# Casting and turning the inputs block by block, with a rearranged opening, in a gated recurrence followed by a maxout layer

## The chip, the cores and the metric

The kernel runs on one core of one Trainium2 chip. The core has five engines, each with its own queue of instructions in program order: TensorE (PE, matrix multiplies), VectorE (DVE), ScalarE (ACT), GpSimd (POOL) and SyncE (SP, which here only issues transfers), and 16 DMA engines that they share. The metric is the time of one execution on the device, in microseconds (us).

## What is computed

`x` and `f_logit` are [4, 6144, 256] in float32, `w1` and `w2` are [256, 1024], `w_out` is [1024, 256].

```python
sig = 1 / (1 + exp(-f_logit))
f = lower_bound + (1 - lower_bound) * sig
i = 1 - f
h = 0
for t in range(6144):                 # for each of 4 sequences, 256 channels
    h = f[:, t] * h + i[:, t] * x[:, t]
    y[:, t] = h
g = maximum(y @ w1, y @ w2)           # y as 24576 tokens of 256
out = g @ w_out
```

The kernel rewrites this. With u = sigmoid(-f_logit), i is (1 - lower_bound) u and f is 1 - (1 - lower_bound) u. The factor (1 - lower_bound), `om` in the code, leaves the recurrence and is multiplied into the weights. The maximum is taken as h1 + relu(h2 - h1): one matmul with `wd` = om (w2 - w1) and a relu, and the linear part y (om w1 w_out) with a 256x256 matrix `w13` that is made once.

## The kernel before

The 24576 tokens are cut into 48 blocks of 512 tokens (`TB`), 12 to a sequence. For the scan and the matmuls a block must lie with its channels on the partitions, so it has to be turned. This is done in two ways.

Blocks 0 to 2 are loaded in float32 with tokens on the partitions (`load`, tiles `fn`, `xn`), gated there (`gate_nat` on ACT makes `un`, `drive_nat` on DVE makes `vn` = un xn) and turned on PE (`turn_pe`). Blocks 3 to 47 go through DRAM. `cast` has POOL issue two DMAs that write bfloat16 copies of the rows, `fs` and `xs`, to a scratch tile in DRAM; `turn_dma` has SP issue two transposing DMAs that bring them back as `fT` and `xT`. Block 3 is a chunk of its own, and then two blocks make a chunk (`CB = 2`). `cast_after_turn` keeps the two apart: POOL first copies one element of the `fT` just being turned into `held`, and so waits until it has landed, before it issues the next cast. The next turn waits for that cast. There are two pairs of scratch tiles (`NS`) and three buffers each for `fT` and `xT` (pool `turned`).

`gate` (ACT) makes `u` from `fT`, `drive` (DVE) makes `v` = u xT, `forget` makes `ff` = 1 - om u, and `scan` (DVE) runs the recurrence over a block, once for each half of the channels, from the last column of the block before.

The main loop runs over blocks j and eight slots `fc`. In a slot PE does `hidden(j, fc)`, two matmuls of 512 columns into a `dT` tile (pool `ps_d`, five banks), and half a token group of `project(j-1, .)`, five matmuls of 256 columns into a `psO` tile (`ps_o`, three banks). ACT turns `dT` into `rt` with the relu. `store` copies a `psO` tile to `osb` on DVE and has SP write it out, twice a block, at `fc` 0 and 4. All orders are written out by hand: `gate_of` says in which slot a block is gated, `turn_of` in which slot a chunk is turned. A gate that waits holds up what is behind it on ACT and DVE, relus among it; a turn that waits holds up the stores behind it on SP.

In the opening the weights come in quarters of their columns. For each quarter `diff` makes w2 - w1, `scale` multiplies by `om` into `wd`, and `turn_w1` turns w1 on PE for the linear matrix (`keep_w1` copies it out, `linear_weights` multiplies, `keep_linear` scales). `keep_warm` issues matmuls without use while data is awaited. At the end the last tokens are stored by `store_row`, one copy half on DVE and half on ACT.

Of the kernel before, what the change touches and what calls it, by code (L numbers as in the profile page):

```python
# [8 lines left out]
FP32 = mybir.dt.float32  # L9
BF16 = mybir.dt.bfloat16  # L10
ALU = mybir.AluOpType
AF = mybir.ActivationFunctionType
# [4 lines left out]
def kernel(  # L17
# [26 lines left out]
    CB = 2  # L44
    assert NBB % CB == 0
    chunks = [(NP, 1)] + [(j, CB) for j in range(NP + 1, NBLK, CB)]
    NCH = len(chunks)
    home = {j + o: (c, o) for c, (j, n) in enumerate(chunks) for o in range(n)}
    NS = 2
# [8 lines left out]
    ttpool = ctx.enter_context(tc.tile_pool(name="turned", bufs=3))  # L58
# [3 lines left out]
    opool = ctx.enter_context(tc.tile_pool(name="opool", bufs=4))  # L62
    PS = bass.MemoryType.PSUM
# [10 lines left out]
    w1n = wpool.tile([P, KC, DFF], FP32)  # L74
    w2n = wpool.tile([P, KC, DFF], FP32)
# [63 lines left out]
    def scan(j, h, t0=0, t1=TB):  # L139
# [18 lines left out]
    rows, chunk = {}, {}  # L158

    spare = {  # L160
        (k, name): scratch.tile([CB * TB, D], BF16, name=f"{name}{k}")
# [4 lines left out]
    def cast(c):  # L166
        j, n = chunks[c]
        b, k = divmod(j, NBB)
        rows[c] = []
        for name, src in (("fs", f_logit), ("xs", x)):  # L170
            t = spare[c % NS, name]
            nc.gpsimd.dma_start(  # L172
                out=t[0 : n * TB, :],
                in_=src[b, k * TB : (k + n) * TB, :],
                max_dma_last_dim=4096,
            )
            rows[c].append(t)

    def turn_dma(c):
        n = chunks[c][1] * TB  # L180
        for s in range(2):
            t = ttpool.tile([P, KC, CB * TB], BF16, name=("fT", "xT")[s])
            chunk[c, s] = t
            nc.sync.dma_start_transpose(out=t[:, :, 0:n], in_=rows[c][s][0:n, :])

    def gate(j):
        c, o = home[j]
        us[j] = midpool.tile([P, KC, TB], BF16, name="u")
        nc.scalar.activation(  # L189
            out=us[j][:],  # L190
            in_=chunk[c, 0][:, :, o * TB : (o + 1) * TB],
            func=AF.Sigmoid,
            scale=-1.0,
        )
        uT[j] = us[j]

    def drive(j):
        c, o = home[j]
        vT[j] = midpool.tile([P, KC, TB], BF16, name="v")
        nc.vector.tensor_tensor(  # L200
            out=vT[j][:],
            in0=us[j][:],
            in1=chunk[c, 1][:, :, o * TB : (o + 1) * TB],
            op=ALU.mult,
        )
# [4 lines left out]
    def unit(fc):  # L210
        return slice(fc * P, (fc + 1) * P)
# [61 lines left out]
    def store(j, g):  # L273
        osb = opool.tile([P, 2, D], FP32, name="osb")
        nc.vector.tensor_copy(out=osb[:], in_=pos[j, g, 0][:])  # L275
        r0 = j * TB + 2 * g * P
        nc.sync.dma_start(
            out=out[r0 : r0 + 2 * P, :].rearrange("(p r) d -> p r d", r=2), in_=osb[:]
        )

    def store_row(j, g, r):
        osb = opool.tile([P, 2, D], FP32, name="osb")
        ps = pos[j, g, r]
        nc.vector.tensor_copy(out=osb[:, 0, 0:P], in_=ps[:, 0, 0:P])
        nc.scalar.copy(out=osb[:, 0, P:D], in_=ps[:, 0, P:D])
        r0 = j * TB + 2 * g * P
        nc.sync.dma_start(
            out=out[r0 : r0 + 2 * P, :].rearrange("(p r) d -> p r d", r=2)[:, r, :],
            in_=osb[:, 0, :],
        )  # L290
# [4 lines left out]
    def weight_load(k, w, src):  # L295
        cols = slice(k * QF, (k + 1) * QF)
        nc.sync.dma_start(  # L297
            out=w[:, :, cols], in_=src[:, cols].rearrange("(h p) f -> p h f", p=P)
        )
# [25 lines left out]
    def scale(k, h):  # L325
        cols = slice(k * QF, (k + 1) * QF)
        nc.scalar.activation(
            out=wd[:, h, cols], in_=wdf[:, h, cols], func=AF.Copy, scale=om[:, h : h + 1]
        )

    pts = {}

    def turn_w1(k):
        pts[k] = ps_d.tile([P, 2, D], FP32, name="dT")
        for q in range(2):
            for h in range(KC):
                nc.tensor.transpose(
                    pts[k][:, q, h * P : (h + 1) * P],
                    w1n[:, h, unit(2 * k + q)],
                    ident[:],  # L340
                )

    def keep_w1(k):
        nc.scalar.copy(out=w1T[:, 2 * k : 2 * k + 2, :], in_=pts[k][:])
# [33 lines left out]
    gate_at = {NP: (1, 7), NP + 1: (3, 2), NP + 2: (3, 6), NP + 3: (5, 0), NP + 4: (5, 5)}  # L378
    gate_at |= {b: (b - 2, 5) for b in range(NP + 5, NBLK)}
    gate_of = {}  # L380
    for b, at in gate_at.items():
        gate_of.setdefault(at, []).append(b)
    turn_of = {(1, 3): 1}
    turn_of |= {(chunks[c][0] - 3, 5): c for c in range(2, NCH)}

    def cast_after_turn(c):

        last = chunks[c - 1][1] * TB - 1
        nc.gpsimd.tensor_copy(out=held[:], in_=chunk[c - 1, 0][:, KC - 1, last : last + 1])  # L389
        cast(c)  # L390

    with tc.manual_schedule():
# [4 lines left out]
        nc.scalar.dma_start(out=lbr[:], in_=lower_bound.rearrange("(h p) -> h p", p=P))  # L397
        load(0, 0, 0, 2)
        load(0, 1, 0, 2, nc.scalar)
        for k in range(2):  # L400
            weight_load(k, w1n, moe_w1)
            weight_load(k, w2n, moe_w2)
            if k == 0:
                load(0, 0, 2, 4)
                load(0, 1, 2, 4)
# [15 lines left out]
        keep_warm(6)  # L421
        keeps()
        keep_warm(2)


        gate_nat(0, 0, 2)
        drive_nat(0, 0, 2)
        for s in range(2):
            for q in range(2):
                turn_pe(0, s, q)  # L430
        forget(0, 0, 0, HB, on_act=True)
        forget(0, 1, 0, HB)
        for h in range(KC):
            scan(0, h, 0, HB)
        diff(0, 0, KC, nc.gpsimd)
        turn_w1(0)
        keep_warm(3)
        gate_nat(0, 2, 4)
        drive_nat(0, 2, 4)
        for s in range(2):  # L440
            for q in range(2, 4):
                turn_pe(0, s, q)
        scale(0, 0)
        forget(0, 0, HB, TB, on_act=True)
        forget(0, 1, HB, TB)
        scale(0, 1)
        keep_w1(0)
        for fc in range(2):
            hidden_cols(0, fc, 0, HB)
        for h in range(KC):  # L450
            diff(1, h, h + 1, nc.gpsimd)
# [3 lines left out]
        for h in range(KC):  # L455
            scale(1, h)
# [6 lines left out]
        keep_w1(1)  # L463
        for h in range(KC):
            diff(2, h, h + 1, nc.gpsimd)
        for h in range(KC):
            scale(2, h)
# [3 lines left out]
        turn_w1(2)  # L471
        for s in range(2, 4):
            for i in range(4):
                project_steps(0, i, s, s + 1)
        keep_w1(2)
        diff(3, 0, KC, nc.vector)
        for h in range(KC):
            scale(3, h)
        for fc in range(4, 6):
            hidden(0, fc, on_dve=(fc == 5))  # L480
        linear_weights(0, 4)
        turn_w1(3)
        gate_nat(1, 0, 2)
        drive_nat(1, 0, 2)
        keep_w1(3)


        for q in range(2):
            turn_pe(1, 0, q)
        for h in range(KC):  # L490
            forget(1, h, 0, HB, on_act=True)
        for fc in range(6, 8):
            hidden(0, fc, on_dve=(fc == 7))
# [14 lines left out]
        forget(1, 0, HB, TB, on_act=True)  # L508
        forget(1, 1, HB, TB)
# [6 lines left out]
        for i in range(4):  # L516
            project_steps(0, i, 8, 10)


        nc.gpsimd.tensor_copy(out=held[:], in_=ins[2][0][:, NQ - 1, D - 1 : D])  # L520
        cast(0)
        turn_dma(0)
        cast_after_turn(1)

        for j in range(1, NBLK + 1):
# [3 lines left out]
            for fc in range(FC):  # L529
                if j < NBLK:  # L530
                    hidden(j, fc, on_dve=(j == 1 and fc % 2 == 1))
# [5 lines left out]
                if j == 1:  # L537
                    if fc == 0:
                        gate_nat(2, 0, NQ)
                        drive_nat(2, 0, NQ)  # L540
                        store(0, 0)
                    if fc == 3:
                        store(0, 1)
                    if fc in (5, 6):
                        for q in range(NQ):
                            turn_pe(2, fc - 5, q)
                    if fc == 7:
                        for h in range(KC):
                            forget(2, h, on_act=True)
                        for h in range(KC):  # L550
                            scan(2, h)
# [15 lines left out]
                c = turn_of.get((j, fc))  # L567
                if c is not None:
                    turn_dma(c)
                    if c + 1 < NCH:  # L570
                        cast_after_turn(c + 1)
# [30 lines left out]
```

## Time and profile before

| | us |
|---|---|
| timed runs, median (lowest to highest of 3) | 402.17 (401.64 to 513.32) |
| the profiled execution | 400.45 |
| its span, first to last instruction | 398.7 |
| PE busy | 389.7 |
| ACT busy | 271.2 |
| DVE busy | 248.7 |
| POOL busy | 46.5 |

The profiled execution is one execution of its own. Its own time is 1.75 us more than its span. A row of a group or of the timeline gives the line of the code, the engine, the operation and what it writes from what. `PEld` is the loading of a stationary operand, `SPq` or `POOLq` an entry of a queue, such as the issue of a DMA. The row marked PE in the slices counts the tenths in which it was busy. A wait names the waiting engine and line, then what it waited for, the total, how many times, and the longest. The granted clock of TensorE was 1.0 throughout.

### The profile page before, as it was taken

To read this page: it belongs to the slowest core of one execution; us is meant where nothing else is said; L and a number is where in the kernel's file an instruction comes from. 1 tells how busy PE (TensorE), PEld (TensorE's weight loads), DVE (VectorE), ACT (ScalarE), POOL (GpSimd) and SP (SyncE) were. 2 spreads that over 40 slices of the span, in tenths; PEclk is the share of its full clock that TensorE was granted. 3 is DMA by queue.
4 is the path that set the end of the run, shared out by engine and by line. 5 is a ranking of instruction groups with operands and counts; after the bars stand their busy time and mean duration, and the time that the engine had idled before them with its cause. 6 is when DMAs were issued, how large, how long until landed. Compare 5 with 4: busy or idle time off the path is not lost.

```text
span 398.7 us, 7240 instructions
## 1 busy us (share of the span) xinstructions
PE 389.7 (98%) x2784; PEld 271.9 (68%) x2784; DVE 248.7 (62%) x353; ACT 271.2 (68%) x450; POOL 46.5 (12%) x82
## 2 busy tenths in 40 slices
PE   7989999999999999999999999999999999999996
PEld 4756676667776677766777667776677766777664
DVE  3677757765676577567656765765676567657621
ACT  3856767667766766676677667666766776676661
POOL 2420111011012020020110110110201101100000
PEclk9999999999999999999999999999999999999999
DMA  8979999999998999999999999999999999895122
GB/s 261 348 162 188 231 221 248 200 220 194 201 223 193 214 191 219 200 177 234 190 186 220 202 187 216 198 217 203 173 238 183 190 218 206 188 213 145 54 103 83
DMA packets 126359, 79.13 MB, mean 198 GB/s; under 512 B 96242, under 2 KB 102644, under 8 KB 126324
## 3 DMA queue, kind: packets, MB, share of 16 engines
q1 hardware_dynamic: 113792, 54.80, 54.2%
q0 software_dynamic: 12256, 23.60, 36.8%
q8 instruction: 22, 0.36, 0.4%
q10 hardware_dynamic: 276, 0.26, 0.2%
q14 instruction: 13, 0.11, 0.1%
HBM read 53.48 MB, written 48.76 MB: 256 GB/s over the span
## 4 chain that ended last, share of the span: by engine, by line
PE 87%; DMA 10%; DVE 1%; POOL 0%; issue 0%; ACTq 0%; SPq 0%; ACT 0%; DVEq 0%; POOLq 0%
PE psO L259 49%; PE dT L221 38%; DMA xs<-in_x_dram 2%; DMA fn<-in_f_logit_dram 2%; DMA w2n<-in_moe_w_dram 2%; DMA xT<-xs 1%; DMA xn<-in_x_dram 1%; DMA fs<-in_f_logit_dram 1%; DMA fT<-fs 1%; DVE y L148 1%; DVE v L200 0%; POOL fs L172 0%; ACTq L397 0%; DVE ff L135 0%; SPq L297 0%
## 5 line engine op out<-in xcount | busy, mean ns | idle before, releaser
L236 ACT ACTIVATE rt<-dT 128x512 bf16<-128x512 f32 x376 | 219.1, 596 | 112.5 <-PE dT L221 111.8
L221 PE MATMUL dT<-y,wd 128*128 128x512 bf16 (+1 forms) x772 | 227.3, 378 | 2.9 <-DVE rt L234 1.4
L259 PE MATMUL psO<-wob,rt 128*128 128x256 bf16 x1536 | 229.0, 273 | 0.2 <-DVE rt L234 0.2
L259 PEld LDWEIGHTS <-rt 128*128 128x128 bf16 x1536 | 150.2, 98 | 96.1 <-DVE rt L234 0.4
L148 DVE TENSOR_TENSOR_SCAN y<-ff,y,v 128x512 bf16<-128x512 bf16 x84 | 107.8, 1283 | 3.0
L200 DVE TENSOR_TENSOR v<-u,xT 128x1024 bf16<-128x1024 bf16 x45 | 31.1, 691 | 100.2 <-ACT u L189 91.7
L221 PEld LDWEIGHTS <-wd 128*128 128x128 bf16 x772 | 75.4, 98 | 15.1 <-issue 3.5
L275 DVE COPY osb<-psO 128x512 f32<-128x512 f32 x95 | 64.3, 678 | 29.2 <-PE psO L259 29.1
L259 PE MATMUL psO<-w,y 128*128 128x256 bf16 x384 | 72.8, 273 | 0.0
L389 POOL CAST held<-fT 128x1 f32<-128x1 bf16 x22 | 14.6, 663 | 286.5 <-DMA fT<-fs 286.5
L189 ACT ACTIVATE u<-fT 128x1024 bf16<-128x1024 bf16 x45 | 47.1, 1047 | 0.0
L259 PEld LDWEIGHTS <-y 128*128 128x128 bf16 x384 | 37.5, 98 | 4.4
L135 DVE TENSOR_SCALAR ff<-u,nom 128x512 bf16<-128x512 bf16 x90 | 30.3, 337 | 0.0
L172 POOL DMA_DIRECT2D fs<-in_f_logit_dram x23 | 12.8, 558 | 1.7 <-issue 1.5
L172 POOL DMA_DIRECT2D xs<-in_x_dram x23 | 12.7, 550 | 0.0
L148 DVE TENSOR_TENSOR_SCAN y<-ff,v 128x512 bf16<-128x512 bf16 x6 | 7.3, 1225 | 0.2
L234 DVE TENSOR_SCALAR rt<-dT 128x512 bf16<-128x512 f32 x8 | 5.3, 686 | 3.2 <-PE dT L221 3.2
L148 DVE TENSOR_TENSOR_SCAN y<-ff,y,dT 128x256 bf16<-128x256 bf16 (+1 forms) x8 | 6.6, 861 | 0.0
L370 PE MATMUL psO<-warm 128*128 128x512 bf16 x11 | 5.3, 629 | 1.2 <-DVE warm L418 1.2
L110 DVE TENSOR_TENSOR vn<-un,xn 128x512 bf16<-128x512 bf16 (+1 forms) x5 | 3.9, 788 | 3.3 <-ACT un L103 2.0
L131 ACT ACTIVATE ff<-dT,nom 128x256 bf16<-128x256 bf16 (+1 forms) x7 | 3.5, 536 | 3.1 <-PE dT L122 3.1
L318 POOL TENSOR_TENSOR wdf<-w2n,w1n 128x256 f32<-128x256 f32 (+1 forms) x5 | 4.1, 837 | 7.5 <-DMA w2n<-in_moe_w_dram 7.5
(34 smaller groups left out, 40.1 us busy)
## 6 DMA issues: line engine op xcount, KB each, us to landing
out_dram<-osb SPq DMA_DIRECT2D x95, 256.0 KB, 3.0
fs<-in_f_logit_dram POOLq DMA_DIRECT2D x22, 512.0 KB, 5.8
xs<-in_x_dram POOLq DMA_DIRECT2D x22, 512.0 KB, 9.2
fn<-in_f_logit_dram SPq DMA_DIRECT2D x4, 256.0 KB, 5.9
w1n<-in_moe_w_dram SPq DMA_DIRECT2D x4, 256.0 KB, 5.8
w2n<-in_moe_w_dram SPq DMA_DIRECT2D x4, 256.0 KB, 6.5
won<-in_moe_w_out_dram SPq DMA_DIRECT2D x2, 512.0 KB, 6.7
xn<-in_x_dram SPq DMA_DIRECT2D x3, 256.0 KB, 6.8
```

Of the source, the lines that this page charges most:

```text
L135: nc.vector.tensor_scalar(out=o, in0=i, scalar1=nom[:, h : h + 1], scalar2=1.0, op0=ALU.mult, op1=ALU.add)
L148: nc.vector.tensor_tensor_scan(out=ys[j][:, h, t0:t1], data0=ffs[j][:, h, t0:t1], data1=vT[j][:, h, t0:t1], initial=initial, op0=ALU.mult, ...
L172: nc.gpsimd.dma_start(out=t[0 : n * TB, :], in_=src[b, k * TB : (k + n) * TB, :], max_dma_last_dim=4096,)
L189: nc.scalar.activation(out=us[j][:], in_=chunk[c, 0][:, :, o * TB : (o + 1) * TB], func=AF.Sigmoid, scale=-1.0,)
L200: nc.vector.tensor_tensor(out=vT[j][:], in0=us[j][:], in1=chunk[c, 1][:, :, o * TB : (o + 1) * TB], op=ALU.mult,)
L221: nc.tensor.matmul(dts[j, fc][:, t0:t1], lhsT=wd[:, kc, unit(fc)], rhs=ys[j][:, kc, t0:t1], start=(t0 == 0 and kc == 0), stop=(t1 == TB an ...
L234: nc.vector.tensor_relu(out=rt[:], in_=dts[j, fc][:])
L236: nc.scalar.activation(out=rt[:], in_=dts[j, fc][:], func=AF.Relu)
L259: nc.tensor.matmul(ps, lhsT=lhsT, rhs=rhs, start=(s == 0 and (r == 0 or alone)), stop=(s == FC + KC - 1 and (r == 1 or alone)), skip_group ...
L275: nc.vector.tensor_copy(out=osb[:], in_=pos[j, g, 0][:])
L370: nc.tensor.matmul(idle[:].rearrange("p r d -> p (r d)"), lhsT=warm[:, 0:P], rhs=warm[:], start=True, stop=True,)
L389: nc.gpsimd.tensor_copy(out=held[:], in_=chunk[c - 1, 0][:, KC - 1, last : last + 1])
```

## The change

Casts and turns go block by block from block 3 on. There are three pairs of scratch tiles and five buffers each for `fT` and `xT`. A turn still waits for its cast, and the next cast for that turn, through `held`. Slots for turns and gates come from a formula: the turn of block b stands 13 slots ahead of its `hidden` at block 6, and the lead grows to 21 slots at block 18 and stays there; the gate stands five slots after the turn. Block 3's cast waits for the second half of block 1's `xn` rather than for block 2's `fn`.

In the opening `lbr` (the lower bound) moves from ACT's queue to SP's, behind the first load. `w1` is rounded to bfloat16 by `round_w1` before it is turned, on POOL for quarters 0, 2 and 3 and on ACT for quarter 1. `scale` runs partly on DVE, `diff` of quarter 2 moves from POOL to DVE and that of quarter 3 from DVE to POOL, some `forget` calls move to ACT, one `keep_w1` to DVE. Block 2 is gated and driven ahead of the main loop, its turning and its two scans are spread over block 1's slots, and block 0's outputs are copied on ACT. At the end, each of the two last rows is copied whole on DVE to a tile of its own.

```diff
-    CB = 2
-    chunks = [(NP, 1)] + [(j, CB) for j in range(NP + 1, NBLK, CB)]
-    NS = 2
+    NS = 3
...
-    ttpool = ctx.enter_context(tc.tile_pool(name="turned", bufs=3))
+    ttpool = ctx.enter_context(tc.tile_pool(name="turned", bufs=5))
...
+    def turn_dma(j):
+        for s, name in enumerate(("fs", "xs")):
+            t = ttpool.tile([P, KC, TB], BF16, name=("fT", "xT")[s])
+            turned[j, s] = t
+            nc.sync.dma_start_transpose(out=t[:], in_=spare[j % NS, name][:])
+
+    def cast_after_turn(j):
+        nc.gpsimd.tensor_copy(out=held[:], in_=turned[j - 1, 0][:, KC - 1, TB - 1 : TB])
+        cast(j)
...
     def store_row(j, g, r):
-        osb = opool.tile([P, 2, D], FP32, name="osb")
-        ps = pos[j, g, r]
-        nc.vector.tensor_copy(out=osb[:, 0, 0:P], in_=ps[:, 0, 0:P])
-        nc.scalar.copy(out=osb[:, 0, P:D], in_=ps[:, 0, P:D])
+        osb = lastpool.tile([P, D], FP32, name="row")
+        nc.vector.tensor_copy(out=osb[:], in_=pos[j, g, r][:, 0, :])
...
+    def round_w1(k, on_act=False):
+        cols = slice(k * QF, (k + 1) * QF)
+        o, i = w1b[:, :, cols], w1n[:, :, cols]
+        if on_act:
+            nc.scalar.copy(out=o, in_=i)
+        else:
+            nc.gpsimd.tensor_copy(out=o, in_=i)
...
-    gate_at = {NP: (1, 7), NP + 1: (3, 2), NP + 2: (3, 6), NP + 3: (5, 0), NP + 4: (5, 5)}
-    gate_at |= {b: (b - 2, 5) for b in range(NP + 5, NBLK)}
...
-    turn_of = {(1, 3): 1}
-    turn_of |= {(chunks[c][0] - 3, 5): c for c in range(2, NCH)}
+    turn_of, gate_of = {(1, 7): [NP + 1], (3, 2): [NP + 2]}, {(1, 7): [NP]}
+    for b in range(NP + 1, NBLK):
+        at = max(FC * (b - 2) + 3 - (2 * (b - 2 * NP)) // 3, FC * (b - 3) + 3)
+        if b > NP + 2:
+            turn_of.setdefault(divmod(at, FC), []).append(b)
+        if b == NP + 1:
+            at -= 3
+        gate_of.setdefault(divmod(at + 5, FC), []).append(b)
...
-        nc.scalar.dma_start(out=lbr[:], in_=lower_bound.rearrange("(h p) -> h p", p=P))
         load(0, 0, 0, 2)
         load(0, 1, 0, 2, nc.scalar)
+        nc.sync.dma_start(out=lbr[:], in_=lower_bound.rearrange("(h p) -> h p", p=P))
...
+        gate_nat(2, 0, NQ)
+        drive_nat(2, 0, NQ)
-        nc.gpsimd.tensor_copy(out=held[:], in_=ins[2][0][:, NQ - 1, D - 1 : D])
-        cast(0)
-        turn_dma(0)
-        cast_after_turn(1)
+        nc.gpsimd.tensor_copy(out=held[:], in_=ins[1][1][:, NQ - 1, D - 1 : D])
+        cast(NP)
+        turn_dma(NP)
+        cast_after_turn(NP + 1)
...
-                    hidden(j, fc, on_dve=(j == 1 and fc % 2 == 1))
+                    hidden(j, fc, on_dve=(j == 1 and fc in (1, 3, 6)))
...
                 if j == 1:
-                    if fc == 0:
-                        gate_nat(2, 0, NQ)
-                        drive_nat(2, 0, NQ)
-                        store(0, 0)
-                    if fc == 3:
-                        store(0, 1)
-                    if fc in (5, 6):
+                    if fc in (0, 2):
                         for q in range(NQ):
-                            turn_pe(2, fc - 5, q)
-                    if fc == 7:
+                            turn_pe(2, fc // 2, q)
+                    if fc == 2:
                         for h in range(KC):
                             forget(2, h, on_act=True)
-                        for h in range(KC):
-                            scan(2, h)
+                    if fc == 3:
+                        scan(2, 0)
+                    if fc == 6:
+                        scan(2, 1)
+                    if fc == 5:
+                        store(0, 0, on_act=True)
+                    if fc == 7:
+                        store(0, 1, on_act=True)
```

## The prediction, made before the changed kernel had run

> **What bounds the kernel now.** I began with busy time and the slices, to see which engine is full, and where.
>
> ```profile
> span 398.7 us, 7240 instructions
> ...
> PE 389.7 (98%) x2784; PEld 271.9 (68%) x2784; DVE 248.7 (62%) x353; ACT 271.2 (68%) x450; POOL 46.5 (12%) x82
> ...
> PE   7989999999999999999999999999999999999996
> ...
> DMA  8979999999998999999999999999999999895122
> ```
>
> PE is full from the third slice to the last. The DMA row is almost as full, so the transfers are the next limit. The chain that ended last gives PE's pace: pieces of the same place in the loop stand exactly one block apart.
>
> ```profile
> 83.88 0.55 PE psO L259 x5
> ...
> 91.70 0.55 PE psO L259 x5
> ```
>
> One block takes 7.82 us: 16 matmuls of 512 columns and 40 of 256, 18,432 columns, 0.424 ns a column. A slot (one `fc`) is 0.977 us. PE has no wait listed after 60 us, so no edit can shorten that stretch. It can only lengthen it. What can be won lies before 47 us and after the last matmul. The waits of PE up to 60 us show how little that is:
>
> ```profile
> PE dT L221 <- DVE rt L234: 1.4, 1, 1.4
> PE psO L370 <- DVE warm L418: 1.2, 1, 1.2
> PE dT L221 <- DVE y L148: 1.0, 3, 0.5
> ```
>
> Last I read the stretch of the one block that already goes alone (chunk 0, block 3), since the change makes every block go that way.
>
> ```profile
> 20.20 0.70 POOL L172 DMA_DIRECT2D fs<-in_f_logit_dram  x1
> ...
> 23.89 1.34 SPq L184 DMA_TRANSPOSE fT<-fs  x1
> ...
> 25.33 1.23 SPq L184 DMA_TRANSPOSE xT<-xs  x1
> ...
> 27.52 0.19 POOL L389 CAST held<-fT 128x1 f32<-128x1 bf16 x1 [6.11 <-DMA fT<-fs]
> ...
> 27.97 0.55 POOL L172 DMA_DIRECT2D fs<-in_f_logit_dram  x1 [0.26 <-issue]
> ```
>
> Cast, landing, transpose, landing, `held`, next cast are strictly serial. This one-block cycle took 27.97 - 20.20 = 7.77 us. The block's matmuls take 7.82. That coincidence decides the case.
>
> **1. Casts and transposes block by block.** Before, 22 cycles of two blocks have 15.64 us each. The median landings are 5.8 us (fs) and 4.5 us (fT); alone, one block took 3.69 from cast to transpose and 3.6 to `held`. So halving the rows does not halve the time: 5.8 + 4.5 = 10.3 us for two blocks becomes 2 x 7.3 = 14.6. `held` and the next issue add about 0.5 each time. Twenty-two more casts and transposes of each kind and 22 more `held` copies are issued (45 blocks against 23 chunks). POOL (12% busy) and SP have room for them; the cycle does not.
>
> The cycle C: 7.77 less 0.15, since later issues take 0.55 and not 0.70, is 7.62 at best. On top comes what block 3 did not meet. Two stores a block pass through the same DMA engines; the loads of the opening, 256 KB like a store, follow each other every 0.75 us, so the two hold the engines up to 1.5 us. In the order of the changed program one store follows each pair of transposes on SP and lands in the gap before the next cast; the other comes four slots later and may hit the cast. I bound this by 0 and 0.75. `held` took 185 to 1171 ns: 0 to 0.98 more; the long ones began during a scan. So C lies between 7.62 and about 9.3, and I take 7.72, near the only row of that shape: SP issues the first store behind xT, while casting has not begun, and a late chain finds DVE waiting rather than scanning.
>
> One rule of the Trainium skill speaks against it. Each GpSimd issue of a cast took 523 to 700 ns in all 46 rows, whatever DVE did beside it. "SBUF — State Buffer", section "🔬 SBUF: two separate sides" (its trap "DVE blocks DMA"), says that GpSimd cannot write descriptors while DVE holds the shared port, and its subsection on bandwidth pools has 620 ns becoming 3100. By the page a cycle that met this each time would be some 2.5 us longer, an estimate from its figures, and the kernel near 500 us; by the rows it costs nothing.
>
> What C costs. The new positions ask for turns every 7.33 slots (7.17 us) from block 6 to 18, then every 8. Slot 24, at 38.07 now, comes at 35.8 (part 2), so slot n is at 35.8 + 0.977(n - 24). SP reaches turn 7 (slot 43) at 54.4 and, after a store, issues it at 55.0. From there the chain runs at C. fT of block 18 lands at 55.0 + 11C + 3.5, and its gate stands at slot 128, 137.4 us, in ACT's queue ahead of the relus. Behind a late gate wait the relus and, on DVE, the output copies; PE can run about 4 us without relus, as five dT banks take five slots less one in work. With C = 7.72 the landing is at 143.4, 2.0 us past 141.4. After block 18 the demand is 7.82 and the lag stops growing. Each C above 7.82 adds 29(C - 7.82). So: C = 7.62 costs 0.9; 7.72, 2.0; 7.9, 6.3; 8.0, 10.3; 8.2, 18.3; below 7.5 nothing. The third scratch tile pair and the five turned buffers cost nothing: a cast still waits for the turn just before it.
>
> **2. The opening.** Up to 18.5 us loads set the pace: they land 0.75 us apart, in nearly the same order, and the last w_out cast (POOL, 17.06 to 18.52) waits for its load. Earlier scaling (second half from ACT to DVE, 0.5 us each), w1 turned in bf16 (before, 16 f32 transposes at 0.11 to 0.22 us) and w1 rounded on POOL and ACT (at most 1.46 us each, by the 128x1024 cast) lie ahead of that cast. The two more warming matmuls fill PE's idle time ahead of data, and `wd` scaled on DVE lies between the rows of 0.34 (ff, 128x256) and 0.69 (128x512). Hidden 0 may start up to 1.5 us earlier and then wait for the same load. The queue order is kept except `lbr`, 1 KB, which moves behind the first load and lets xn start 0.55 us earlier. Bounds: 0.5 lost (POOL now rounds three of the quarters) and 0.5 won (that cast at 1.04, as its first half); I take 0.
>
> From 22.45 to 38.07 PE does 32 matmuls of 512, 40 of 256 and 16 transposes of 128 columns, 28,672 columns, 12.2 us, in 15.6. Of the 3.4 us lost, some 0.65 (block 1's last scan) stays, because that scan has the same place. The rest is DVE's: it did vn of block 2 (1.23) and two output copies (0.68 each) ahead of the relus and the scan. The change puts vn before block 1's hidden part, the copies on ACT (ACT now: 0.6 each, and the gate of block 3 behind them), and a third relu and the two scans apart. Of 2.75 I count 2.3 won; bounds 0.5 (ACT late instead, two copies and one `un` of 1.05) and 3.
>
> **3. Casting block 3 earlier.** `held` waits for block 1's x, not block 2's logits: 18.5 against 20.0 us, and POOL is free at 18.5. This starts the chain up to 1.4 us earlier. It buys slack already used above; block 4's wait for xT (two-block transfer, 0.3 us of PE) goes.
>
> **4. Last rows.** DVE copied half (0.29), then ACT half (0.27), one behind the other: the store went 0.61 after the copy began. One copy of 256 columns lies between 0.29 and 0.68; at 0.42 the end comes 0.2 earlier.
>
> **Sum.** 398.7 - 2.3 - 0.2 + 2.0 = 398.2 span. The profiled execution took 400.45, 1.75 more than its span, so 400.0. The median of the timed runs, 402.17, stands 1.7 above the profiled one, which would make 401.7; I say 401.
>
> **Rivals.**
> - *The DMA chain becomes the bound.* For: DMA row at 9, and a stock cycle of 7.77 without stores. Against: no excess is seen where one block went alone. If a store meets the cast in two blocks of three, C = 8.2: 398.2 + 16.3 + 1.75 = 416. It decides from C = 8.0 (408.3, about 2% over 400.45). Place: from block 18 on, ACT's gate waiting for fT. Chance 0.33.
> - *The chain is quicker than its first cycle,* C at most 7.5, as the first landing still had loads beside it: 396.2 + 1.75 = 398. Against: fixed parts of 10.3 against 14.6 above. Chance 0.15.
> - *The opening gives nothing,* relus now late on ACT: 2.3 more, 402.3. Chance 0.10.
> - Forecast, C from 7.5 to 8.0: 0.42.
>
> **How the numbers follow.** About 2% (8 us) is what a measurement of this kernel can tell from no change. To be faster by that, 8 of some 13 us in which PE did no useful work would have to go (last matmul ends at 394.75; 48 blocks make 375.4, transposes and the linear weights of the opening some 6), and more than half of the 13 wait for the first loads: 0.03. The forecast, the second and third rivals and the lower end of C make up 0.64 for within 2% (0.67 less that 0.03). Slower: 0.33. The range goes from 397.5 (second rival) to 416 (first rival at C = 8.2), with its tail above left out.
>
> **What would show it.** Casts should follow each other 7.7 to 7.9 us apart; PE's waits after 60 us should stay a few us and have ACT's relu as releaser, behind a gate that waits for fT. Slot 24 should come at 35 to 36.5. If casts stand over 8 us apart, PE idles in each block and the first rival holds; a wrong bound on PE's cover for a late gate, or `held` near 1 us in each cycle, would make me wrong.

## The result

| | us, median (lowest to highest) | ratio to before, 95% interval |
|---|---|---|
| before | 401.9 (400.67 to 513.32, 4 runs) | 1 |
| after | 450.36 (449.38 to 453.16, 4 runs) | 1.1228 (1.1161 to 1.1296) |

The changed kernel is 12% slower; the ratio leaves out the one run of the kernel before that took 513.32 us. The prediction, 401 us with a range up to 416, was wrong. The case that came true was its first rival, the DMA chain as the bound, and with a cycle longer than the one priced there.

The page of the changed kernel: the lines that answer to those of before, the two groups that wait longest, and the DMA issues.

```profile
span 447.6 us, 7423 instructions
...
PE 395.7 (88%) x2738; PEld 270.0 (60%) x2786; DVE 245.2 (55%) x352; ACT 252.4 (56%) x450; POOL 63.7 (14%) x151
...
PE   6899988598998869989988989988898898998897
...
DMA  7979999778877799899798888987988799989622
...
DMA packets 128472, 79.14 MB, mean 177 GB/s; under 512 B 98354, under 2 KB 104756, under 8 KB 128436
...
DMA 73%; PE 8%; issue 6%; ACT 5%; DVE 4%; SPq 2%; POOL 1%; POOLq 0%; ACTq 0%; DVEq 0%
...
L185 ACT ACTIVATE u<-fT 128x1024 bf16<-128x1024 bf16 x45 | 47.6, 1058 | 154.7 <-DMA fT<-fs 154.7
...
L180 POOL CAST held<-fT 128x1 f32<-128x1 bf16 x44 | 8.1, 183 | 326.7 <-DMA fT<-fs 326.7
...
out_dram<-osb SPq DMA_DIRECT2D x95, 256.0 KB, 2.5
fs<-in_f_logit_dram POOLq DMA_DIRECT2D x45, 256.0 KB, 4.1
```

The lines of before that these are read against:

```profile
DMA packets 126359, 79.13 MB, mean 198 GB/s; under 512 B 96242, under 2 KB 102644, under 8 KB 126324
...
PE 87%; DMA 10%; DVE 1%; POOL 0%; issue 0%; ACTq 0%; SPq 0%; ACT 0%; DVEq 0%; POOLq 0%
...
L389 POOL CAST held<-fT 128x1 f32<-128x1 bf16 x22 | 14.6, 663 | 286.5 <-DMA fT<-fs 286.5
L189 ACT ACTIVATE u<-fT 128x1024 bf16<-128x1024 bf16 x45 | 47.1, 1047 | 0.0
```

PE is no longer full: 8s and single 5s and 6s stand where 9s stood. The chain that ended last has gone over to DMA, 73% of the span where PE had 87%. DMA itself is not fuller. Its row fell, and it moved the same 79.1 MB at 177 GB/s on average against 198. This points to the order of the transfers in time as the bound, and not to their amount; the experiments test it. ACT waits 154.7 us for `fT` in its gates, where before it waited for none. POOL waits 326.7 us in `held`, but it already waited 286.5 before, without harm.

The waits of the changed kernel, of PE and then of SP's queue, say who passes this on (engine and line, what it waited for, total, times, longest):

```profile
ACT u L185 <- DMA fT<-fs: 154.7, 44, 5.2
...
PE dT L216 <- ACT rt L231: 32.4, 28, 2.3
...
SPq L176 <- DMA fs<-in_f_logit_dram: 174.3, 38, 8.5
SPq L275 <- DVE osb L273: 62.3, 14, 6.6
```

A turn waits on SP for its cast (174.3 us), a gate on ACT for the turn, the relus stand behind the gate, and PE waits for them. Before, turns had waited for their casts 13.4 us in all:

```profile
SPq L184 <- DMA fs<-in_f_logit_dram: 13.4, 2, 9.5
```

### The profile page after: what moved, and what is told of

The parts are those of the page before. It is cut to its first block, busy times and chain, and to the rows that moved or that the text cites. A ratio compares the mean times of both kernels' runs of the same rounds, so it can differ in the third digit from the quotient of the medians.

```text
span 447.6 us, 7423 instructions
## 1 busy us (share of the span) xinstructions
PE 395.7 (88%) x2738; PEld 270.0 (60%) x2786; DVE 245.2 (55%) x352; ACT 252.4 (56%) x450; POOL 63.7 (14%) x151
## 4 chain that ended last, share of the span: by engine, by line
DMA 73%; PE 8%; issue 6%; ACT 5%; DVE 4%; SPq 2%; POOL 1%; POOLq 0%; ACTq 0%; DVEq 0%
DMA fs<-in_f_logit_dram 34%; DMA fT<-fs 33%; PE psO L254 5%; ACT rt L231 3%; PE dT L216 3%; DMA xn<-in_x_dram 2%; DMA xT<-xs 2%; ACT u L185 2%; DMA w1n<-in_moe_w_dram 2%; DVE y L145 1%; POOL held L180 1%; SPq L176 1%; DVE v L195 1%; DVE osb L273 1%; DVE ff L132 1%
## 5 line engine op out<-in xcount | busy, mean ns | idle before, releaser
L216 PE MATMUL dT<-y,wd 128*128 128x512 bf16 (+1 forms) x724 | 218.9, 380 | 35.0 <-ACT rt L231 32.4
L254 PE MATMUL psO<-wob,rt 128*128 128x256 bf16 x1536 | 231.8, 274 | 9.9 <-ACT rt L231 6.8
L231 ACT ACTIVATE rt<-dT 128x512 bf16<-128x512 f32 x377 | 195.0, 610 | 26.0 <-PE dT L216 24.7
L185 ACT ACTIVATE u<-fT 128x1024 bf16<-128x1024 bf16 x45 | 47.6, 1058 | 154.7 <-DMA fT<-fs 154.7
L273 DVE COPY osb<-psO 128x512 f32<-128x512 f32 x93 | 59.4, 674 | 14.4 <-PE psO L254 14.4
L180 POOL CAST held<-fT 128x1 f32<-128x1 bf16 x44 | 8.1, 183 | 326.7 <-DMA fT<-fs 326.7
L166 POOL DMA_DIRECT2D fs<-in_f_logit_dram x45 | 23.4, 520 | 11.7 <-issue 11.4
L166 POOL DMA_DIRECT2D xs<-in_x_dram x45 | 23.2, 516 | 0.3 <-DMA xT<-xs 0.3
L128 ACT ACTIVATE ff<-dT,nom 128x256 bf16<-128x256 bf16 (+1 forms) x10 | 4.6, 513 | 1.3 <-PE dT L119 1.2
L100 ACT ACTIVATE un<-fn 128x512 bf16<-128x512 f32 (+1 forms) x5 | 3.6, 714 | 2.9 <-DMA fn<-in_f_logit_dram 2.9
```

Of the source, the lines that this page charges most:

```text
L166: nc.gpsimd.dma_start(out=spare[j % NS, name][:], in_=src[b, k * TB : (k + 1) * TB, :], max_dma_last_dim=4096,)
L180: nc.gpsimd.tensor_copy(out=held[:], in_=turned[j - 1, 0][:, KC - 1, TB - 1 : TB])
L185: nc.scalar.activation(out=us[j][:], in_=turned[j, 0][:], func=AF.Sigmoid, scale=-1.0,)
L216: nc.tensor.matmul(dts[j, fc][:, t0:t1], lhsT=wd[:, kc, unit(fc)], rhs=ys[j][:, kc, t0:t1], start=(t0 == 0 and kc == 0), stop=(t1 == TB an ...
L231: nc.scalar.activation(out=rt[:], in_=dts[j, fc][:], func=AF.Relu)
L254: nc.tensor.matmul(ps, lhsT=lhsT, rhs=rhs, start=(s == 0 and (r == 0 or alone)), stop=(s == FC + KC - 1 and (r == 1 or alone)), skip_group ...
```

## How the time goes round

The casts of the changed kernel, from POOL's timeline (start, duration, instruction, in brackets the idle time before it):

```profile
84.21 0.18 POOL L180 CAST held<-fT 128x1 f32<-128x1 bf16 x1 [8.17 <-DMA fT<-fs]
84.66 0.52 POOL L166 DMA_DIRECT2D fs<-in_f_logit_dram  x1 [0.26 <-issue]
...
93.68 0.18 POOL L180 CAST held<-fT 128x1 f32<-128x1 bf16 x1 [8.00 <-DMA fT<-fs]
94.12 0.52 POOL L166 DMA_DIRECT2D fs<-in_f_logit_dram  x1 [0.27 <-issue]
...
103.35 0.18 POOL L180 CAST held<-fT 128x1 f32<-128x1 bf16 x1 [8.20 <-DMA fT<-fs]
```

One block's cycle takes 9.5 to 9.7 us here, where PE needs a block every 7.82. Over all 44 cycles the mean is 8.91 us. The issues and landings in the trace take it apart (means in us):

| | before, block 3 alone | after | no stores | constant lead |
|---|---|---|---|---|
| cast issued to fs landed | 3.67 | 4.30 | 3.75 | 4.51 |
| fs landed to turn issued | 0.02 | 0.41 | 0.15 | 0.17 |
| turn issued to fT landed | 3.52 | 3.65 | 3.80 | 3.83 |
| fT landed to next cast | 0.57 | 0.58 | 0.58 | 0.58 |
| mean cycle | 7.77 | 8.91 | 8.28 | 9.08 |

The last two columns belong to experiments below. A cycle of 8.91 against the 7.82 at which PE would have set the pace, 43 times after the cast of block 4, is 47 us. The span came out 447.6 - 398.2 = 49.4 us above the forecast's. So the cycle is nearly the whole miss.

## The experiments

My theory after the result: casting and turning block by block makes a serial loop (cast, landing, turn, landing, `held`, next cast) that no longer fits into a block's 7.82 us. Rivals: the rearranged opening costs time; single-block transfers cost DMA throughput; the advancing slots of the turns cost the time through the order of the queues; the stores in that loop do.

**The opening alone** (`chunks_new_opening`). The changed kernel with the chunks, slots and turns of the kernel before.

```diff
 # from the changed kernel
-    NS = 3
+    CB = 2
+    chunks = [(NP, 1)] + [(j, CB) for j in range(NP + 1, NBLK, CB)]
+    NS = 2
...
-                for b in turn_of.get((j, fc), []):
-                    turn_dma(b)
+                c = turn_of.get((j, fc))
+                if c is not None:
+                    turn_dma(c)
```

> The changed kernel with the casts, turns and slots of the kernel before (chunks of two blocks), so with the new opening and last rows alone. If casting block by block makes the loss, the loop runs at 7.82 us a block again and the time is that of the kernel before less what the opening wins: the changed profile reaches slot 24 at 36.3 us instead of 38.0, so 398 to 401 us. If the opening or the last rows lose time, it stays clearly above 402 us.

Measured: 399.76 us, ratio 0.9968 (0.9949 to 0.9987). So the opening and the last rows win 0.3%, and all of the loss is the block-by-block part's.

```profile
span 398.4 us, 7192 instructions
...
PE   8899999999999999999999999999999999999996
...
PE 81%; DMA 16%; issue 1%; ACT 1%; SPq 0%; POOL 0%; DVE 0%; POOLq 0%; ACTq 0%
```

PE is full again, from the third slice on.

**The blocks alone** (`blocks_old_opening`). The kernel before with the changed kernel's `cast`, `turn_dma`, `cast_after_turn`, buffers and slots.

```diff
 # from the kernel before
-    CB = 2
-    NS = 2
+    NS = 3
...
-    ttpool = ctx.enter_context(tc.tile_pool(name="turned", bufs=3))
+    ttpool = ctx.enter_context(tc.tile_pool(name="turned", bufs=5))
```

> The kernel before with only the casts, turns and slots of the change. If these make the whole loss, 449 to 454 us, with casts 8.9 us apart. If the loss needs the new opening too, clearly below 445 us.

Measured: 457.43 us, ratio 1.1402 (1.1338 to 1.1465), casts 9.02 us apart. The part makes the loss by itself. It lies some 3 us above what I had expected: 43 cycles, each 0.1 us longer, make about 5 us. The two runs behind it, 455.27 and 459.60 us, are 4 us apart.

**Without the stores** (`no_stores`). The output transfers of blocks 3 to 45 are left out, so most of `out` is never written; the copies to `osb` stay.

```diff
+        if j < NP or j >= NBLK - 2:
             nc.sync.dma_start(
                 out=out[r0 : r0 + 2 * P, :].rearrange("(p r) d -> p r d", r=2), in_=osb[:]
             )
```

> The changed kernel without the output transfers of blocks 3 to 45; the copies to osb stay. Theory of the serial chain alone: a cycle without stores takes 7.6 to 7.8 us, as block 3's did before, so PE sets the pace and the time is 397 to 405 us. If the chain itself is 8.9 us without any help from the stores, the time stays at 440 us or more. In between: part of the 1.2 us that a cycle takes more than 7.72 comes from the stores, by colliding with a cast or by holding SP.

Measured: 419.49 us, ratio 1.0456 (1.0425 to 1.0487). It fell between the two, as the third case. From the sixth cycle on the casts are 8.12 us apart, against 8.88 in the changed kernel, so the stores are worth 0.76 us a cycle. From there on the mean landing of the cast fell by 0.67 (4.30 to 3.63) and the turn's wait by 0.28 (0.42 to 0.14), while the turn itself took 0.20 more (3.58 to 3.78). The single casts of the changed kernel agree, from block 8 on: 24 had two stores issued in the 2 us ahead of them and none until they landed, which took 4.41 us on average; eight had one store ahead, 3.61 us; seven had one ahead and another while they ran, 4.97 us. But 8.12 is still over 7.82. Quiet cycles of this run look like this:

```profile
83.55 0.18 POOL L180 CAST held<-fT 128x1 f32<-128x1 bf16 x1 [6.36 <-DMA fT<-fs]
84.00 0.52 POOL L166 DMA_DIRECT2D fs<-in_f_logit_dram  x1 [0.26 <-issue]
...
91.38 0.19 POOL L180 CAST held<-fT 128x1 f32<-128x1 bf16 x1 [6.35 <-DMA fT<-fs]
91.82 0.52 POOL L166 DMA_DIRECT2D fs<-in_f_logit_dram  x1 [0.26 <-issue]
```

That is 7.82 us with no store in the way and nothing waiting: POOL starts `held` on the landing, and SP issues the turn 0.14 us after the cast has landed. Such a cycle just fills a block. The 44 cycles of this run go from 7.17 to 10.48 us, and the mean is higher than 7.82 since in some cycles the turn or the cast lands about a microsecond later; by what, these runs do not show.

**A release one block earlier** (`cast_one_earlier`). The cast of block b+1 waits for the turn of block b-1 instead of that of block b, so casts and turns run beside each other.

```diff
-        nc.gpsimd.tensor_copy(out=held[:], in_=turned[j - 1, 0][:, KC - 1, TB - 1 : TB])
+        if j - 2 >= NP:
+            nc.gpsimd.tensor_copy(out=held[:], in_=turned[j - 2, 0][:, KC - 1, TB - 1 : TB])
         cast(j)
```

> The changed kernel, with the cast of block b+1 released by the turn of block b-1 instead of that of block b (the third pair of scratch tiles has room for it). If the serial order of cast and turn is the bound, the cycle falls below 7.82 us, PE sets the pace, and the time is 397 to 405 us. If the DMA engines are short of throughput (their busy share is 0.8 to 0.9, and casts then run beside turns), the time stays above 430 us.

Measured: 415.47 us, ratio 1.0346 (1.0329 to 1.0363): neither. From block 17 to 43 each `hidden` starts 7.82 us after the one before it, one gap of 7.93 excepted, so there the serial loop was the whole loss. Throughput falls as a rival: 200 GB/s were moved between 140 and 380 us, where the changed kernel moved 178 between 140 and 420. The rows of these stretches, first this run's and then the changed kernel's, give for each engine busy time and instructions, and at the end PE's clock, DMA's busy share and GB/s:

```profile
140.00:380.00 240.00, 234.56 (x1646) 164.27 (x1675) 151.48 (x213) 162.88 (x272) 37.58 (x90) 0.99 1.08 200
...
140.00:420.00 280.00, 250.59 (x1742) 173.05 (x1772) 157.14 (x222) 155.92 (x283) 37.35 (x93) 1.00 0.87 178
```

About 21 us still go before block 17, where up to 16 us lie between the starts of two blocks instead of 7.82. The long gaps, from block 8 to block 16, lie where the advancing turns (of blocks 6 to 18) stand. On SP's queue the stores now wait most:

```profile
SPq L276 <- DVE osb L274: 151.1, 73, 9.9
SPq L176 <- DMA fs<-in_f_logit_dram: 14.0, 5, 9.3
```

That total alone proves little, since before the change stores waited 212.9 us there without harm. The written order explains it. In some of those blocks a store's slot comes to stand between the gate of block b and the turn of block b+1. The store waits for a DVE copy, the copy stands behind the whole gate on DVE, and the gate waits for `fT` of block b. So the turn of b+1, behind that store on SP, cannot start before block b is gated, scanned and copied. By the slots this concerns, among the advancing turns, those of blocks 9, 10, 11, 15, 16 and 17. In this run these six were issued 7.7 to 14.0 us after their casts had landed, and the others from block 7 to 18 at most 5.7. In the changed kernel just these were issued 1.7 to 2.1 us after it, and no other turn after block 5 more than 0.2.

The changed kernel's DVE and SP between its casts at 84.66 and 94.12 show the loop:

```profile
85.28 0.69 DVE L195 TENSOR_TENSOR v<-u,xT 128x1024 bf16<-128x1024 bf16 x1 [4.63 <-ACT u L185]
...
87.83 1.28 DVE L145 TENSOR_TENSOR_SCAN y<-ff,y,v 128x512 bf16<-128x512 bf16 x1
89.03 0.67 DVE L273 COPY osb<-psO 128x512 f32<-128x512 f32 x1
...
89.72 0.34 SPq L275 DMA_DIRECT2D out_dram<-osb  x1
90.24 1.30 SPq L176 DMA_TRANSPOSE fT<-fs  x1
```

The cast had landed at 88.17. The turn went at 90.24, when the gate's scans, the copy and the store were through.

**Slots at a constant lead** (`constant_lead`). The changed kernel with every turn from block 6 on 13 slots ahead, at `fc` 3, with no store between a gate and the next turn.

```diff
-        at = max(FC * (b - 2) + 3 - (2 * (b - 2 * NP)) // 3, FC * (b - 3) + 3)
+        at = FC * (b - 2) + 3 + (2 if b == NP + 1 else 1 if b == NP + 2 else 0)
```

> The changed kernel with turns 13 slots ahead of their block throughout, every 8 slots, at fc 3, so that no store stands in SP's order between a block's gate and the next turn. The casts wait as in the change. If the serial loop of cast, turn and held is what binds after block 18 (8.9 us with stores, 8.1 without), removing the six late turns (blocks 9 to 11 and 15 to 17, 2 us behind their casts) and the earlier gates wins some 10 to 20 us of the 49 lost: 425 to 440 us, casts 8.3 to 8.9 us apart. If the advancing slots were the whole cause, 398 to 403 us.

Measured: 448.24 us, ratio 1.1174 (1.1106 to 1.1242). Both expectations missed. The late turns are gone (0.17 us from landing to turn), but the cast now lands after 4.51 us, and the cycle is 9.08. The gain went into the landings of the cast and of the turn. A likely cause is that the stores that wait behind a turn on SP are issued together, just ahead of the next cast: so it was for 32 of the 40 casts from block 8 on, against 24 in the changed kernel.

```profile
188.49 1.23 SPq L176 DMA_TRANSPOSE fT<-fs  x1
189.81 1.25 SPq L176 DMA_TRANSPOSE xT<-xs  x1
191.15 1.00 SPq L275 DMA_DIRECT2D out_dram<-osb  x2
```

POOL issued the next cast at 192.63; it landed 4.24 us later, the one after it (at 202.03, again behind two stores) 5.80. While the loop is serial, the slots win nothing that stands clear of the noise: the two intervals overlap.

**Both** (`constant_lead_earlier`).

```diff
 # cast_one_earlier, and
-        at = max(FC * (b - 2) + 3 - (2 * (b - 2 * NP)) // 3, FC * (b - 3) + 3)
+        at = FC * (b - 2) + 3 + (2 if b == NP + 1 else 1 if b == NP + 2 else 0)
```

> The same slots, and the cast of block b+1 released by the turn of block b-1. In the run with that alone, block after block took 7.82 us from block 18 on, and 20 us went between blocks 7 and 18, where slots advance. If these are the two causes and there is no third, the time is 397 to 401 us. If single-block transfers cost throughput as well, it stays above 405 us.

Measured: 401.51 us, ratio 1.0001 (0.9981 to 1.0022), half a microsecond above the range I had given. Two edits bring the time back to that of the kernel before. They do not bring it below: with the same opening, chunks of two blocks took 399.76. So going block by block wins nothing here even when the loop is open. The four kernels make a square: with the release of the change, advancing slots 450.36 and constant ones 448.24; with the earlier release 415.47 and 401.51. The release, serial and now once for each block, is the cause, and the slots count only once the loop is open.

**lbr on POOL's queue** (`constant_lead_earlier_lbr`, `chunks_lbr`, and the latter again beside its twin).

```diff
-        nc.sync.dma_start(out=lbr[:], in_=lower_bound.rearrange("(h p) -> h p", p=P))
+        nc.gpsimd.dma_start(out=lbr[:], in_=lower_bound.rearrange("(h p) -> h p", p=P))
```

> The same again, with lbr loaded from POOL's queue instead of SP's. In the changed kernel the load of the second quarter of w2 is issued at 4.76 us (3.81 before), as it waits for the first load, and every later load lands 0.7 us later than before. If lbr's place does that, loads land 0.7 us earlier again and the time falls by 0.5 to 1 us against the run without it; if the opening is not bound by loads, nothing changes.

> The new opening on chunks of two blocks (399.76 us, ratio 0.9968), with lbr loaded from POOL's queue. By the same reasoning 0.5 to 1 us less: 398.8 to 399.3 us, unless the cast chain of block 4 (0.7 us of PE lost there) takes the gain.

Measured: 401.8 us, ratio 1.0018 (0.9994 to 1.0041), and 399.58 us, ratio 0.9964 (0.9947 to 0.9981): no difference from the kernels without the edit, so both expectations of a gain missed. The waits of `constant_lead_earlier_lbr` show what the release and the slots together changed in the loop. In the changed kernel ACT waited 154.7 us for `fT` and SP 174.3 for the casts:

```profile
ACT u L186 <- DMA fT<-fs: 17.4, 17, 2.1
...
SPq L176 <- DMA fs<-in_f_logit_dram: 12.1, 5, 9.0
```

I ran the second pair once more, both openings side by side.

> The new opening on chunks of two blocks once more, beside the next kernel on the same chip: 399.5 to 400 us, ratio to the kernel before 0.995 to 0.998.

> The same with lbr on POOL's queue. Its profile showed loads landing 0.7 us earlier and a span of 397.2 us against 398.4. If the opening is bound by its loads, the ratio is 0.002 to 0.003 lower than without it; if the gain is lost behind them, both ratios agree within 0.001.

Measured: 400.2 us, ratio 0.9974 (0.9959 to 0.9990), and 399.67 us, ratio 0.9970 (0.9953 to 0.9986). The ratios agree within 0.001. The loads do land 0.9 us earlier (last quarter of w2 at 13.82 us against 14.72, in the first pair's profiles), but `hidden` of block 1 starts at 23.35 against 23.50, and in the second pair's traces at 23.61 against 22.51. The gain is lost between the loads and block 1. Both versions beat the kernel before by 0.3%, and I know of no better one.

## Why the prediction was wrong

**What bounds the kernel** held: PE before, DMA next, and the 7.77 us cycle against 7.82 as the point on which the case turns.

**Part 1, the cycle C, is the step that failed.** I took 7.72, from the one cycle with a single block; it measured 8.91. Two terms were mis-sized. The stores, bounded by 0 and 0.75 and taken near 0, cost 0.76, the whole of my bound. My reason, that SP issues the first store behind xT while casting has not begun, describes what happens, but a late loop mostly puts both stores there, directly ahead of the cast (24 of the 40 casts from block 8 on). The rest of the cycle, taken as 7.62, was 8.12 without stores. The 0.15 that I took off for shorter issues was not there, as a cast still landed 3.63 us after its issue began, against 3.67 for block 3's. SP issued the turn 0.14 and not 0.02 after the landing, and the turn took 3.78 on average and not 3.52. One sample stood near the lower end of the distribution: 36 of the 44 cycles without stores were longer than block 3's. The third term, `held`, was rightly put near nothing: it took 183 ns.

The trace of before had a better row, which I did not use: the two-block cycles of its start, when it was late and the loop nearly set its own pace, stores included. The turns in these two cycles were issued 0.14 and 0.89 us after their casts had landed, the second behind a store.

```profile
40.78 0.55 POOL L172 DMA_DIRECT2D fs<-in_f_logit_dram  x1 [0.26 <-issue]
...
54.36 0.55 POOL L172 DMA_DIRECT2D fs<-in_f_logit_dram  x1 [0.26 <-issue]
...
67.78 0.55 POOL L172 DMA_DIRECT2D fs<-in_f_logit_dram  x1 [0.26 <-issue]
```

These take 13.5 us for two blocks. Splitting adds what does not halve. Estimated from the median landings it is 2 x 3.7 - 5.8 = 1.6 for the cast, 2 x 3.5 - 4.5 = 2.5 for the turn and 0.6 for `held`. That is 18.2 us for two blocks, 9.1 for one. Measured: 8.9. The closeness is partly luck: with the landings of these two cycles themselves (6.4 and 7.0 for the cast, 6.4 and 4.9 for the turn) the same sum gives 8.0. Either way C lies above 7.82 and the loop sets the pace.

A rule of the Trainium skill points the same way. "DMA: Bandwidth & Descriptors", section "🔬 Anatomy of one DMA — SWDGE (gpsimd) path", gives each DMA on that path a fixed cost of about 2.0 us. The estimate from the medians is 1.6 for the cast, and 2.5 for the turn, which is not of that path.

**The price of C** was nearly right. Put 8.9 into the prediction's own terms: the landing of block 18's `fT` at 156.4 is 15 us late, 29 x 1.08 adds 31, and the span is 396.2 + 46 = 442. It was 447.6. The formula's start is where it fell short: turn 7 was issued at 61.2 and not 55.0, as the cycles of blocks 4 to 6 already took 9.4 to 10.3 us. With 61.2 in its place the same terms give 449.

**The slots.** I counted them as a demand on the chain and overlooked that an advancing turn passes a store. In the changed kernel this cost nothing that lasts; with the loop open it cost 14 us.

**The skill's rule on GpSimd's port,** weighed in part 1, did not show: the 90 issues of casts took about 520 ns each, `held` 183, beside a DVE that was scanning a quarter of the time. The page speaks of one mode of DVE operations, and no run here shows which of these operations use it.

**Part 2, the opening,** came close. From the start of `hidden` of block 1 to that of block 3 before took 15.5 us and after 13.4, so 2.1 won of the 2.3 forecast. But `hidden` of block 1 started 0.5 us late, at 23.0 and not 22.5, the lower end of my bounds. One trace tells little of it: in the seven traces with this opening the start lies between 22.5 and 24.2. The cause stays open. POOL's rounding is hardly it: having rounded, POOL in the changed kernel still waited 0.16 us for the load of w2's last quarter. The loads do come later. The first load and xn now start together, and the first lands at 4.38 us in `chunks_new_opening` and not at 3.54; the load of w2's second quarter waits for it since `lbr` has another place. But in the three traces with `lbr` on POOL's queue, with earlier loads, block 1 starts at 23.3 to 23.7. The delay is there by the time ACT starts `un` of block 1 (16.4 to 18.4 us in these ten traces), and `hidden` of block 1 follows 5.8 to 6.1 us later in each. **Part 3** gave the earlier start (19.46 against 20.20), and the loop used it up. **Part 4** was right: the last store was issued 0.49 us after the last matmul and not 0.66, 0.17 won against 0.2.

**The rivals.** The first came true, at 450 and not 416: its price rested on C = 8.2, a store meeting the cast in two blocks of three. Its place came true too: ACT's gate waits for `fT`. The second (a quicker chain) and the third (nothing from the opening) were wrong.

## What to carry to other kernels

A loop of transfers in which each waits for the landing of the last costs its fixed parts once per turn; before halving the pieces, take the pace of the loop where it runs late and loaded, and add the parts that do not halve. When DMA looks full and order might be the bound, let one transfer start a step earlier: if the same bytes then move faster, it was the order. When entries are written to several in-order queues by hand, look between a gate and the next transfer for an entry that waits for that gate.

## What was unexpected of the hardware

The DMA engines, 0.9 busy by the profile, were not short of throughput. With casts and turns side by side, in the trace of `constant_lead_earlier_lbr`, a cast took 5.35 us to land and a turn 6.82 on average, against 4.30 and 3.65 in series, and yet all but a few blocks went through at 7.82 us and not 8.91.
